# Split operands for the second half of group 1's output projections in a fused attention and FFN kernel

## The chip, the cores and the metric

One core of a Trainium2 chip runs the whole program. The metric is the device time of one execution in microseconds (us); three runs of the kernel before gave a median of 738.64 us (738.53 to 738.88). Engines are called as the profile calls them: PE (TensorE matmul), PEld (its weight load), DVE (VectorE), ACT (ScalarE), POOL (GpSimd), SP (SyncE, which issues the DMAs).

## The reference, cut to what matters

Attention over 4 batches of 8 heads, 768 positions, head size 64, where a query sees a window of 128 positions and 4 sink positions. Its output, as 3072 tokens of 512 features, goes through a feed-forward block:

```
h  = x @ w_in                      # 3072x512 @ 512x2048
sp = maximum(h, 0) + log1p(exp(-abs(h)))
g  = h * erf(sp)
out = g @ w_out                    # 3072x2048 @ 2048x512, float32
```

All inputs and the output are float32.

## The kernel before, in words

**Tiling.** The tokens are cut into 12 groups of 256 (`GT`), each group two halves of 128. `DF` = 2048 is cut into 16 blocks `f` of 128 (`NF` = 16). One step `m` is one block of one group: `g, f = divmod(m, NF)`, so group 0 is m = 0 to 15, group 1 is 16 to 31, group 2 begins at 32. In each step `hidden` (L638) makes h for block f (contraction over four c of 128 features), on odd steps `act` (L650) turns two blocks of h into g, and `project` (L678) adds the block of step m - `LAG` (`LAG` = 4) to the two output accumulators of its group.

**Attention** runs ahead of the feed-forward work in steps `s`, four head pairs to a group, one about every four m. A step is `core(s)` (L302: `av` of step s - 2, then the scores), softmax on DVE and ACT (`norm`, L371), `ptrans(s)` (L391: transposes on PE, copies on ACT, masks on POOL) and `xfin` (L459), which writes slice c of the group's x as xh (rounded) and xl (rest). So group g's four slices become complete one after another, and the last, c = 3, lets the hidden matmuls of that group finish.

**Two ways to multiply in float32.** Unsplit operands are float32 and a product is one `matmul` of the program (two instructions in the profile: L641, L687). Split operands are pairs of type float32r, a rounded part and the rest, and a product is three matmuls (L645; L690, L691, L692). Weights arrive as `ws`, are rearranged to float32 `wf` on DVE (`wconv`, L533) and are split into `wt` by `wsplit` (L555): a copy on ACT (L560) makes the rounded part, a subtraction on DVE (L561) the rest. Blocks 0 to 15 are of w_in, 16 to 31 of w_out. Group 0's hidden products are unsplit, those of all other groups split. The projections of groups 0 and 1 are unsplit (`whole` in `act`), those of groups 2 to 11 are split. For a split projection `act` ends with a cast on DVE (L674, gh) and a subtraction on POOL (L675, gl); for an unsplit one it ends with the float32 tile gf.

**What sets the order.** Each engine executes its own list in order. A planner makes these lists when the program is built: it takes ready instructions by a key, 256 times the step plus an offset by kind (`O`, L45: `act` -400, `core` -300, `ptrans` -200, `hid` 0, `ws` 300, `res` 500, `proj` 900; smaller goes first), so projections are what PE takes when nothing else is ready. `follow` (L278) adds an order between two instructions of one engine. `split` (L520) says at which m each weight block is split; L559 puts the split behind the last square and the last product of an earlier `act`. `project` gets a function (L602) that orders the first matmul of a *split* projection behind the last hidden matmul of the same step m, where that step's group is 2 or more and f is not 0. The unsplit branch (L686 to L688) does not use it. Hidden blocks 2k and 2k + 1 share one PSUM bank; the trace has the second one's matmuls behind the first one's.

**Buffers that matter here.** `g` has 2 (gf or gh with gl), `u` 4, PSUM `h`, `o` and `t` 2 each, the weights share 33.

Of the kernel before, what the change touches and what calls it, by code (L numbers as in the profile page):

```python
# [39 lines left out]
NE, AL = 4, 2  # L40

NM, NA = 2, 8

PW, EA = 256, 12
O = dict(prep=-100, norm=-100, core=-300, av=-300, load=-400, dup=-100, kcopy=-50, ptrans=-200, xfin=-100,  # L45
# [7 lines left out]
def kernel(  # L53
# [17 lines left out]
    NF = DF // P  # L71
# [59 lines left out]
    def fast_path():  # L131
        with ExitStack() as st:
# [145 lines left out]
            def follow(prev, ins):  # L278

                if prev is not None:  # L280
                    tc.add_manual_dep(
                        ins.ins, prev.ins.name,
                        mybir.DependencyInfo(mybir.DependencyClass.NoSync, mybir.DependencyReason.DATA), reason="order",
                    )
                return ins
# [188 lines left out]
            def at(a, what):  # L474

                key = int(a * PW) + O[what] + (E.get(what, 0) if a < EA else 0)
                return tc.high_priority(offset=tc.tile_snap_priority() + 1 - key)

            def pos(s):

                return s if s < NE else 3 * s - 6 if s < 2 * NPAIR else 4 * s - 11

            plan = {}
            for s in range(NSTEP + AL):
# [15 lines left out]
                if s < 2 * NPAIR:  # L500
                    x = pos(s) + (3 if s < NE else 5)
# [6 lines left out]
            def attn(a):  # L508

                for what, fn, s in sorted(plan.get(a, ()), key=lambda x: (STAGES.index(x[0]), x[2])):  # L510
                    with at(a, what):
                        fn(s)
# [3 lines left out]
            def need(n):  # L516
                return 4 * (n // 4) if n < 16 else n - 16 + LAG

            order = sorted(range(32), key=need)
            split = {}  # L520
            for n in range(32):
                split.setdefault(NF - 5 + n if n < 16 else 2 * NF - 8 + (n - 16) * 3 // 2, []).append(n)

            def wload(n):

                src = wblock(n)
                t = staged[n] = wpool.tile([P, 2 * DM], I32, tag="wo", name=f"ws_{n}")
                if src.dtype == F32:
                    nc.sync.dma_start(t[:, :DM].bitcast(F32), src)
                else:  # L530
                    nc.sync.dma_start(t, src.bitcast(I32))

            def wconv(n, wn):  # L533

                s = staged.pop(n)
                if wn % 2 == 0:
                    wpair.append(wpool.tile([P, 2, DM], F32, tag="wo", name=f"wf_{n}"))
                t = wf[n] = wpair[-1][:, wn % 2]
                if wblock(n).dtype == F32:
                    nc.vector.tensor_copy(t, s[:, :DM].bitcast(F32))  # L540
                    return
                w, ti = s.rearrange("p (n t) -> p n t", t=2), t.bitcast(I32)
                first = nc.vector.tensor_scalar(
                    ti, w[:, :, 1], 0x07FFFFFF, 3, op0=ALU.bitwise_and, op1=ALU.logical_shift_left
                )
                follow(mark["s", 2] if wn < 1 else mark["t", 3] if wn < 3 else mark["s", 3], first)
                follow(mark.get(("c", wn - 2)), first)
                nc.vector.scalar_tensor_tensor(
                    out=ti, in0=w[:, :, 1], scalar=-0x40000000, in1=ti, op0=ALU.bitwise_and, op1=ALU.bitwise_or
                )  # L550
                mark["c", wn] = nc.vector.scalar_tensor_tensor(
                    out=ti, in0=w[:, :, 0], scalar=29, in1=ti, op0=ALU.logical_shift_right, op1=ALU.bitwise_or
                )

            def wsplit(n, m):  # L555

                t = wf[n]
                d = wt[n] = wpool.tile([P, 2, DM], F32R, tag="wo", name=f"wt_{n}")
                x, y = mlp.mark[(m - 1) // 2 - 1]  # L559
                follow(x, nc.scalar.copy(d[:, 0, :], t))  # L560
                follow(y, nc.vector.tensor_tensor(d[:, 1, :], t, d[:, 0, :].bitcast(F32), op=ALU.subtract))  # L561

# [6 lines left out]
            mlp = make_mlp(work, ps_h, ps_o)  # L569
            wn, wl = 0, W0  # L570
            gs = {}
# [15 lines left out]
            for m in range(-LEAD, NG * NF + LAG + 2):  # L587
                a = m + LEAD
                live = 0 <= m < NG * NF
                if live:  # L590
                    g, f = divmod(m, NF)
                    if f % 2 == 0:
                        hp = mlp.hid_tile(m)
                    if f > 0:
                        with at(a, "hid"):
                            ahead = mlp.hidden(hp, xp[g], f)
                attn(a)
                w = m - LAG
                if 0 <= w < NG * NF:
                    g2, f2 = divmod(w, NF)  # L600
                    with at(a, "proj"):
                        mlp.project(gs[w // 2], g2, f2, lambda ins: follow(ahead if live and f and g >= 2 else None, ins))  # L602
                    if f2 == NF - 1:
                        for i in range(2):
                            r0 = (g2 * 2 + i) * P
                            with at(a, "res"):
                                nc.sync.dma_start(out[r0 : r0 + P, :], mlp.result(g2, i))
                if live:
                    if f == 0:
                        with at(a, "hid"):  # L610
                            mlp.hidden(hp, xp[g], f)
                    if f % 2 == 1:
                        with at(a, "act"):
                            gs[m // 2] = mlp.act(hp, m, g < 2)

                while wn < 32 and a >= 1 and (wn < (0, 0, 3, 5)[a - 1] if a < 5 else wn < 2 * a - 4 or need(order[wn]) <= m + W1):
                    with at(a, "wc"):
                        wconv(order[wn], wn)
                    wn += 1
                    with at(a, "wl"):  # L620
                        for n in order[wl : wn + WQ]:
                            wload(n)
                            wl += 1
                for n in split.get(m, ()):
                    with at(a, "ws"):
                        wsplit(n, m)
# [72 lines left out]
    def general_path():  # L699

        NT_S = S // P
        with ExitStack() as st:
# [71 lines left out]
            with tc.tile_pool(name="g_one1", bufs=1) as one, tc.tile_pool(name="g_work1", bufs=2) as work:  # L774
# [3 lines left out]
                with tc.For_i(0, B, 1) as b:  # L778
                    for gb in range(GPB):
# [25 lines left out]
                        for i in range(2):  # L805
# [3 lines left out]
                            )  # L809

    fast_path()
    ok = nc.values_load(flagi[0:1, 0:1], min_val=0, max_val=1)
    with tc.If(ok == 0):  # L813
# [31 lines left out]
```

## Time and profile before

| | value |
|---|---|
| median of 3 runs | 738.64 us (738.53 to 738.88) |
| profiled execution, device time | 738.16 us |
| its span in the trace | 736.5 us (1.66 us lie around it) |
| PE busy | 716.0 us, 97% |
| PEld busy | 595.6 us, 81% |
| ACT busy | 551.9 us, 75% |
| DVE busy | 485.3 us, 66% |
| POOL busy | 210.1 us, 29% |
| mean granted PE clock | 0.997 |

A matmul's listed duration contains its pipeline and overlaps the next one; what one costs in a row of them is the distance between starts. The profiled execution is 0.48 us below the median of the runs.

### The profile page before, as it was taken

How to read it: one execution, taken by the hardware profiler on the slowest of the kernel's cores; microseconds unless marked ns; L12 is line 12 of the kernel's file. 1: busy time of each engine (PE TensorE's matmuls, PEld its weight loads, DVE VectorE, ACT ScalarE, POOL GpSimd, SP SyncE). 2: the span in 40 equal slices, each digit the busy share in tenths (PEclk: the TensorE clock that was granted, in tenths of full speed). 3: DMA queues.
4: the chain of work that ended last, by engine and by line, in shares of the span. 5: the costliest groups of instructions: out<-in, count | busy, mean ns of one | idle time of the engine just before them, and what ended most of it. 6: DMA issues, size and time to landing. Idle time of an engine off the chain costs nothing. (4 is left out here: it accounts for less than half of the span.)

```text
span 736.5 us, 16405 instructions
## 1 busy us (share of the span) xinstructions
PE 716.0 (97%) x5808; PEld 595.6 (81%) x5808; DVE 485.3 (66%) x1367; ACT 551.9 (75%) x1313; POOL 210.1 (29%) x302
## 2 busy tenths in 40 slices
PE   6889999999999999999999999999999999999997
PEld 3666567767888888888888888888898888898885
DVE  7999997665776765665666666665566566475252
ACT  4687759976986876976976975985886886777573
POOL 3411332111323322332333232233224223233221
PEclk9999999999999999999999999999999999999999
DMA  7999011121222122212212211311321221200000
GB/s 175 279 347 377 22 37 55 31 57 40 72 48 69 45 54 48 65 43 57 67 41 56 75 38 44 84 36 40 78 48 37 79 58 35 67 13 2 29 1 34
DMA packets 113001, 53.07 MB, mean 72 GB/s; under 512 B 91728, under 2 KB 105552, under 8 KB 112912
## 3 DMA queue, kind: packets, MB, share of 16 engines
q1 hardware_dynamic: 112352, 51.87, 26.3%
q8 instruction: 49, 0.80, 0.5%
q14 instruction: 40, 0.33, 0.1%
q10 hardware_dynamic: 560, 0.07, 0.1%
HBM read 38.01 MB, written 6.29 MB: 60 GB/s over the span
## 5 line engine op out<-in xcount | busy, mean ns | idle before, releaser
L645 PE MATMUL h<-xh,wt 128*128 128x256 f32 x1408 | 277.9, 285 | 0.2 <-DVE u L667 0.2
L645 PEld LDWEIGHTS h<-xh,wt 128*128 128x128 f32 x1408 | 224.0, 188 | 7.6 <-issue 1.7
L675 POOL TENSOR_TENSOR g<-u,g 128x512 fp32r<-128x512 f32 x80 | 106.2, 1327 | 339.3 <-DVE g L674 335.4
L645 PE MATMUL h<-xl,wt 128*128 128x256 f32 x704 | 198.2, 282 | 0.0
L663 ACT ACTIVATE u<-r 128x512 f32<-128x512 f32 x288 | 161.5, 622 | 12.7 <-DVE gf L667 4.7
L645 PEld LDWEIGHTS h<-xl,wt 128*128 128x128 f32 x704 | 132.2, 188 | 5.0 <-issue 1.2
L667 DVE SCALAR_TENSOR_TENSOR u<-u,u 128x512 f32<-128x512 f32 x160 | 124.5, 778 | 16.0 <-ACT u L663 1.8
L691 PE MATMUL o<-wt,g 128*128 128x512 f32 x320 | 127.4, 398 | 0.0
L690 PE MATMUL o<-wt,g 128*128 128x512 f32 x320 | 127.3, 398 | 0.0
L692 PE MATMUL o<-wt,g 128*128 128x512 f32 x320 | 123.6, 397 | 0.2 <-POOLq L813 0.2
L667 DVE SCALAR_TENSOR_TENSOR u<-u,h 128x512 f32<-128x512 f32 x80 | 54.9, 686 | 84.5 <-ACT u L663 82.3
L416 POOL TENSOR_SCALAR_AFFINE_SELECT pz<-pa 64x256 f32<-64x256 f32 (+1 forms) x96 | 54.5, 567 | 150.8 <-ACT pa L405 147.5
L367 ACT ACTIVATE pst<-pst,neg 128x144 f32<-128x144 f32 x192 | 77.4, 407 | 24.9 <-DVE neg L363 23.9
L658 ACT ACTIVATE r<-h 128x512 f32<-128x512 f32 x96 | 56.7, 591 | 17.9 <-PE h L645 14.4
L690 PEld LDWEIGHTS o<-wt,g 128*128 128x128 f32 x320 | 60.0, 187 | 11.5 <-ACT ot L696 0.4
L692 PEld LDWEIGHTS o<-wt,g 128*128 128x128 f32 x320 | 59.0, 188 | 12.5 <-POOLq L813 0.7
L691 PEld LDWEIGHTS o<-wt,g 128*128 128x128 f32 x320 | 60.0, 188 | 10.5
L674 DVE CAST g<-u 128x512 fp32r<-128x512 f32 x80 | 34.6, 432 | 46.3 <-PE o L692 43.6
L659 ACT ACTIVATE r<-r 128x512 f32<-128x512 f32 x96 | 60.7, 632 | 2.5
L660 ACT ACTIVATE r<-r 128x512 f32<-128x512 f32 x96 | 60.7, 632 | 2.5
L687 PE MATMUL o<-wf,gf 128*128 128x512 f32 x128 | 58.3, 594 | 1.2 <-DVE gf L667 1.2
L297 ACT COPY kq<-tqk 128x512 f32<-128x512 f32 x48 | 27.9, 582 | 32.6 <-PE tqk L294 30.2
(88 smaller groups left out, 939.2 us busy)
## 6 DMA issues: line engine op xcount, KB each, us to landing
ws<-in_moe_w_in_dram SPq DMA_DIRECT2D x16, 512.0 KB, 6.0
ws<-in_moe_w_out_dram SPq DMA_DIRECT2D x16, 512.0 KB, 8.3
out_dram<-ot SPq DMA_DIRECT2D x24, 256.0 KB, 2.1
v<-in_v_dram SPq DMA_DIRECT2D x56, 96.0 KB, 2.2
q<-in_q_dram SPq DMA_DIRECT2D x80, 64.0 KB, 2.1
k<-in_k_dram SPq DMA_DIRECT2D x80, 64.0 KB, 2.1
vz<-v SPq DMA_DIRECT2D x80, 64.0 KB, 2.1
kq<-kq SPq DMA_DIRECT2D x28, 64.0 KB, 2.0
```

What stands on the lines that cost most here:

```text
L367: nc.scalar.activation(y, y, AF.Exp, bias=d["neg"][:, i, h : h + 1], scale=-1.0, accum_out=d["sum"][:, i, h : h + 1])
L645: last = nc.tensor.matmul(o, wt[NC * j + c][:, p, fs], xt[e][:, c, :], start=(m == 0), stop=(m == len(ops) - 1))
L658: nc.scalar.activation(r, h, AF.Tanh, bias=b_t, scale=0.5)
L659: nc.scalar.activation(r, r, AF.Square, bias=b_v, scale=-0.5)
L660: nc.scalar.activation(r, r, AF.Square, bias=b_r)
L663: sq = nc.scalar.activation(u, r, AF.Square, bias=b_a[i], scale=CS)
L667: pr = nc.vector.scalar_tensor_tensor(out=acc, in0=u, scalar=CC[i] * CS**2, in1=x, op0=ALU.add, op1=ALU.mult)
L675: nc.gpsimd.tensor_tensor(gl, acc, gh.bitcast(F32), op=ALU.subtract)
L687: nc.tensor.matmul(o, gt[0][:, ws], wf[16 + f], start=(f == 0), stop=(f == NF - 1))
L690: behind(nc.tensor.matmul(o, gh[:, ws], wt[16 + f][:, 0, :], start=(f == 0), stop=False))
L691: nc.tensor.matmul(o, gh[:, ws], wt[16 + f][:, 1, :], start=False, stop=False)
L692: nc.tensor.matmul(o, gl[:, ws], wt[16 + f][:, 0, :], start=False, stop=(f == NF - 1))
```

## The change

Group 1's activations of blocks f = 8 to 15 (m = 25, 27, 29, 31) give split operands, and the projections of these blocks, done at m = 28 to 35, use the split weights 24 to 31. The eight blocks 24 to 31 are split first, at m = 22, 23, 24, 25, 27, 28, 29, 30; blocks 16 to 23 at m = 31, 31, 32, 33, 33, 34, 35, 35, all behind the activation of m = 31 or an earlier one. Before, blocks 16 to 31 were split in order at m = 24, 25, 27, 28, 30, 31, 33, 34, 36, 37, 39, 40, 42, 43, 45, 46. The splits of blocks 0 to 15 keep their places (m = 11 to 26).

```diff
 NM, NA = 2, 8
+
+FH = 8
...
             for n in range(32):
-                split.setdefault(NF - 5 + n if n < 16 else 2 * NF - 8 + (n - 16) * 3 // 2, []).append(n)
+                x = n - 16
+                split.setdefault(NF - 5 + n if x < 0 else NF + 6 + (x - FH) * 5 // 4 if x >= FH else 2 * NF - 1 + x * 2 // 3, []).append(n)
...
                 t = wf[n]
                 d = wt[n] = wpool.tile([P, 2, DM], F32R, tag="wo", name=f"wt_{n}")
-                x, y = mlp.mark[(m - 1) // 2 - 1]
+                x, y = mlp.mark[min((m - 1) // 2, NF) - 1]
                 follow(x, nc.scalar.copy(d[:, 0, :], t))
...
                     if f % 2 == 1:
                         with at(a, "act"):
-                            gs[m // 2] = mlp.act(hp, m, g < 2)
+                            gs[m // 2] = mlp.act(hp, m, m < NF + FH)
```

## Rows read from the trace of the kernel before

**Rows 1.** Windows: us, busy and count of PE, PEld, DVE, ACT, POOL, PEclk, DMA, GB/s.
```profile
160.00:174.00 14.00, 14.00 (x87) 7.82 (x86) 5.21 (x18) 5.37 (x18) 1.42 (x5) 1.00 0.18 41
174.00:190.00 16.00, 14.53 (x131) 12.63 (x130) 10.58 (x43) 15.36 (x43) 2.68 (x6) 1.00 0.36 93
```

**Rows 2.** Waits of PE, 120 to 215 us (three) and 215 to 736 us (one).
```profile
PE av L453 <- ACT pz L411: 0.7, 1, 0.7
PE tp L398 <- DVE pst L382: 0.5, 1, 0.5
PE h L645 <- DVE u L667: 0.2, 1, 0.2
...
PE o L692 <- POOLq L813: 0.2, 1, 0.2
```

**Rows 3.** Timeline of PE: unsplit projections of group 1, and what follows them.
```profile
130.51 7.03 PE L687 MATMUL o<-wf,gf 128*128 128x512 f32 x16
137.38 0.60 PE L398 MATMUL tp<-ident,pst 128*128 128x128 f32 x4
```

**Rows 4.** Timeline of PE: first of 16 split projection matmuls, and what follows them.
```profile
203.80 0.40 PE L691 MATMUL o<-wt,g 128*128 128x512 f32 x1
...
207.53 0.28 PE L645 MATMUL h<-xh,wt 128*128 128x256 f32 x1
```

**Rows 5.** Timeline of PE where group 1 ends: scores 12, projections, av 11, scores 13 and 14.
```profile
157.67 0.85 PE L345 MATMUL ps<-kq 64*64 64x144 f32 x16
...
168.37 3.60 PE L687 MATMUL o<-wf,gf 128*128 128x512 f32 x8
171.90 0.67 PE L453 MATMUL av<-pa,v 128*64 128x64 f32 x12
...
172.96 0.85 PE L345 MATMUL ps<-kq 64*64 64x144 f32 x16
...
180.38 0.85 PE L345 MATMUL ps<-kq 64*64 64x144 f32 x16
```

**Rows 6.** Timeline of PE where group 2 ends: av 15, first projection behind group 3's hidden matmuls.
```profile
226.89 0.55 PE L453 MATMUL av<-pa,v 128*64 128x128 f32 x8
...
232.78 0.40 PE L690 MATMUL o<-wt,g 128*128 128x512 f32 x1
```

**Rows 7.** Source lines: count, duration ns min/median/max, first and last start.
```profile
L560 ACT CAST wt<-wf x32: 600/612/634, 89.4 to 209.6; 128x512 fp32r<-128x512 f32 x32
...
L561 DVE TENSOR_TENSOR wt<-wf,wt x32: 676/685/901, 92.7 to 211.3; 128x512 fp32r<-128x512 f32 x32
...
L674 DVE CAST g<-u x80: 410/427/528, 183.3 to 727.5; 128x512 fp32r<-128x512 f32 x80
...
L675 POOL TENSOR_TENSOR g<-u,g x80: 1278/1295/1672, 183.9 to 728.1; 128x512 fp32r<-128x512 f32 x80
```

**Rows 8.** Timeline of ACT where group 1 ends; idle before in brackets.
```profile
160.31 1.12 ACT L560 CAST wt<-wf 128x512 fp32r<-128x512 f32 x2
...
161.91 0.42 ACT L367 ACTIVATE pst<-pst,neg 128x144 f32<-128x144 f32 x1
...
168.51 0.59 ACT L405 COPY pa<-tp 128x512 f32<-128x512 f32 x1 [4.90 <-PE tp L398]
```

**Rows 9.** Timeline of DVE where group 1 ends; idle before in brackets.
```profile
163.65 0.17 DVE L374 TENSOR_SCALAR sum<-sum 128x4 f32<-128x4 f32 x1 [3.32 <-ACT pst L367]
...
165.31 0.28 DVE L386 TENSOR_TENSOR snk<-pst,sum 128x128 f32<-128x128 f32 x1
...
173.49 0.42 DVE L472 TENSOR_TENSOR xl<-av,xh 128x256 fp32r<-128x256 f32 x1 [5.37 <-ACT xh L471]
```

**Rows 10.** Timelines of DVE and POOL: four softmax scalings without and with POOL's subtraction beside them.
```profile
177.18 0.88 DVE L382 TENSOR_SCALAR pst<-pst,sum 128x128 f32<-128x128 f32 x4
...
206.41 1.93 DVE L382 TENSOR_SCALAR pst<-pst,sum 128x128 f32<-128x128 f32 x4
...
206.37 1.30 POOL L675 TENSOR_TENSOR g<-u,g 128x512 fp32r<-128x512 f32 x1 [3.28 <-DVE sum L375]
```

## The prediction

> **What bounds the kernel now.** I read the windows first. Where group 1 ends, PE is busy for the whole 14.00 us of the stretch 160 to 174 while ACT and DVE work 5.37 and 5.21 us; in the next 16 us PE is busy 14.53 us and ACT, with 15.36 us, is nearly full [rows 1]. The granted clock is 1.00, the 2.4 GHz level, in both. Next come the waits: from 120 to 215 us PE waited three times, 0.7, 0.5 and 0.2 us, 1.4 us together and all of it between 174 and 190, and from 215 to 736 us it waited 0.2 us [rows 2]. So from 120 us on the time is PE's work. What PE no longer has to do comes off the end, unless it waits more elsewhere, and after 215 us nothing is there to take it back. The question is the stretch 150 to 190, where the change lies. Last I read the timeline of that stretch, because there the order of the lists can open a wait that no total shows.
>
> **PE: the products themselves.** 16 instructions of the unsplit form took from 130.51 to 137.38, 0.429 us each, and a product is two of them: 0.859 us [rows 3]. 16 of the split form took from 203.80 to 207.53, 0.233 us each, and a product is three: 0.699 us [rows 4]. The change turns 8 blocks times 2 halves, 16 products, from the one to the other: 16 x 0.160 = **2.55 us** less. All of it lies in the part where PE has no wait, so I count it in full.
>
> The Trainium skill gives other spacings: by "FP8 and Floating Point Precision", section TensorE Precision Notes, true FP32 takes 4 passes, and by "TensorE: Matmul & The Clock Gate", section Back-to-back issue gap, an isolated matmul of 512 columns takes about 216 ns. An estimate from these two pages is 16 x (4 - 3) x 0.216 = 3.5 us less. The rows agree for the unsplit form (0.859 against 0.864) and not for the split one (0.699 against 0.648), so the sum goes by the rows.
>
> **DVE, ACT and POOL: what is added.** Four activations get a cast on DVE, 0.427 us, and a subtraction on POOL, 1.295 us [rows 7]: 1.7 and 5.2 us. POOL is busy 1.42 us in 160 to 174 [rows 1], so its part is hidden unless the projection stands right behind it. It comes three to four steps behind its activation (`LAG`), so it does not; only the last pair (f = 14, 15) is close, and that pair is moved later (below). No split is added; all 32 stay. But 21 of them now lie in m = 22 to 35 instead of 13, that is 8 casts of 0.61 us on ACT and 8 subtractions of 0.69 us on DVE [rows 7], 4.9 and 5.5 us by their durations, taken out of m = 36 to 46. Three of the eight come in among group 1's activations (m = 22 to 30 hold 13 splits instead of 10), where PE had no wait that they could lengthen [rows 1, 2]; five come in behind the last of them (m = 31 to 35 hold 8 instead of 3). There ACT stood idle 4.90 us before its copy at 168.51 [rows 8], and DVE 3.32 and 5.37 us [rows 9]. That is the cover, and I cost the move at nothing; without cover it is the third rival. In return ACT, 15.36 of 16 us busy in 174 to 190, loses casts there. No DMA is added or moved, and the SP queue is as before.
>
> One row speaks against more work for POOL: the four scalings of a softmax step took 0.88 us alone and 1.93 us when POOL's subtraction began at the same moment [rows 10]. So each of the four new subtractions may cost DVE 0 to 1.06 us. The Trainium skill has this as a rule ("SBUF — State Buffer", section Who interferes with whom): a DVE instruction in a two-port mode and a GpSimd instruction block each other for a whole instruction. The trace agrees. On the path it costs 0, or 1.06 us if one hits the softmax of step 12; I take 0, as DVE has 8.7 us of idle time around it [rows 9].
>
> **PE: the order, which is the real risk.** A split projection's first matmul goes behind the last hidden matmul of its step if that step's group is 2 or more and f is not 0. For f = 13, 14, 15 of group 1 the steps are m = 33, 34, 35, that is hidden blocks 1 to 3 of group 2. Unsplit they were free of this. Before, f = 14 and 15 were done from 168.37 on [rows 5] and f = 13 shortly ahead, while nothing else was ready until step 11's av (171.90), which gives the last slice of group 2's x. After the change they cannot be done until that slice is there. So PE loses work with which it bridged that wait. How long is the hole? The round from scores 12 (157.67) to scores 13 (172.96) lasted 15.3 us and PE was busy throughout [rows 1, 5]. Take out three unsplit blocks (3 x 1.72 = 5.2) and the saving of f = 10 to 12 (3 x 0.32 = 1.0): PE has 9.1 us of work left in it. What else must pass in that round is softmax, transposes, copies, av. The next round, 13 to 14, did the same in 7.4 us [rows 5]; then there is no hole. As round 12 ran, the sums came at 163.65 [rows 9], late because ACT did two split casts at 160.31 ahead of the exponentials at 161.91 [rows 8]. The last scaling ended at 165.6 [rows 9], 7.9 us after the scores. Behind it stand the transposes (0.60 [rows 3]), the copies on ACT (0.59 for the first [rows 8], I take twice that for all) and av (171.90 to 172.96, 1.06 [rows 5]), 2.9 us, with handovers 3.1 as an estimate: 11.0 us from scores to scores, a hole of 1.9 us. So **0 to 1.9 us**. The boundary of groups 2 and 3 has this same order already: the blocks behind group 3's hidden matmuls begin at 232.78, after av 15 at 226.89 [rows 6], and PE has no wait there [rows 2]. That pulls towards 0, ACT's casts towards 1.9; I take 0.9.
>
> **PE: what comes back.** The three blocks, now 3 x 1.40 = 4.2 us, are done after the last slice, in 174 to 190, where PE waited 1.4 us [rows 2] for a chain through ACT and DVE that now also has fewer splits beside it. Between 0 and 1.4 us come back; as three times as much work as wait is put there, I take 0.8.
>
> **One wait is added behind this.** Group 1's accumulators are finished later, so their two copies on ACT (like the copy of 0.59 us [rows 8]) come closer to group 2's first projection, which needs those banks. Behind that projection PE still has hidden matmuls of the next pair; 0 to 1.2 us, taken as 0.
>
> **The sum.** 2.55 - 0.9 + 0.8 = 2.45 us less. The profiled execution, 738.16 us (a span of 736.5 and 1.66 around it), would become 735.7. It is 0.48 us under the median of the runs, 738.64, so against the median I forecast **736.2 us**, 0.33% less.
>
> **The rivals.** *The waits go too* (chance 0.12): no hole, and all 1.4 us of waits vanish: 738.64 - 2.55 - 1.4 = 734.7. For it speaks that the split projections no longer hold a `g` buffer from the first product on, only from the cast, so PSUM tiles come free earlier. Against it: those waits are for a softmax chain that is no shorter.
>
> *The hole eats it* (0.20): hole 1.9 us, nothing comes back: 738.0, and with half of the accumulator wait 738.6. For: two casts stood ahead of exponentials before, and more casts are in that stretch now. Then the change does not do what it says in effect: PE works 2.55 us less and waits as much longer, no difference. Against: rows 6.
>
> *Splits in front of the softmax* (0.08, slower): the eight casts of blocks 16 to 23 become ready together behind the last activation. If ACT's list has them ahead of step 12's exponentials or its copies (rows 8 show two so placed), av 11 comes later by 0.56 us each, with nothing left for PE. All eight, 4.5 us on top of the 1.9, give 738.64 - 2.55 + 6.4 = 742.5. It is slower than now once hole and casts pass 2.55 us, and measurably so, past 740.1, beyond 4.0 us, when four of the eight stand there. Against: their key is the largest of those on ACT except the result copies, so they go in only when nothing else is ready in the planner's clock.
>
> **How the numbers follow.** The forecast has 0.60, with its own range 735.0 to 737.2 (hole 0 to 1.9, back 0 to 1.4, not both at the bad end). Two runs of this kernel can be told apart from about 0.2%, 1.48 us: below 737.16 is faster, above 740.12 slower. Faster is 0.60 + 0.12 and 0.02 of the second rival, 0.74; same 0.18; slower 0.08. For 8 in 10 the range reaches from the first rival's full gain to the second's end, 734.4 to 738.6; the third rival, the edge of the second and a gain beyond the first stay out.
>
> **What would show it.** Right: 96 L687 instructions instead of 128, 336 instead of 320 of each of L690 to L692, 84 casts at L674; PE busy about 2.5 us less; the blocks f = 13 to 15 after group 2's first hidden matmuls; L560 ending by about 175 us instead of 209.6; no PE wait after 215 us. The hole would be a wait of PE on L453 or L398, released by ACT or DVE, between 160 and 172. Wrong: a PE wait there of over 2 us with casts L560 ahead of L367 or L405 on ACT (third rival), split products at another spacing than 0.233 us, or new waits at later group boundaries.

## The result and the profile after

The changed kernel takes 744.1 us (median of 4 runs, 743.07 to 744.9) against 738.59 us of the kernel before on the same chip: ratio 1.0072, 95% interval 1.006 to 1.0085. It is **slower by 5.5 us**, where 736.2 was forecast and 738.6 was the end of the range. The profiled execution, 743.62 us with a span of 742.0, stands for it.

The page says what was computed and not where the time is: PE is busy 715.8 us (716.0 before), although 16 products went to the cheaper form. The windows place it (us, busy and count of PE, PEld, DVE, ACT, POOL, PEclk, DMA, GB/s):

```profile
150.00:160.00 10.00, 10.00 (x60) 8.70 (x59) 9.28 (x25) 9.73 (x25) 1.97 (x2) 1.00 0.26 57
160.00:174.00 14.00, 8.68 (x68) 6.28 (x66) 7.82 (x28) 5.49 (x18) 3.44 (x6) 0.76 0.18 40
174.00:190.00 16.00, 15.76 (x157) 13.68 (x158) 7.24 (x24) 12.69 (x33) 4.62 (x11) 0.89 0.31 82
190.00:210.00 20.00, 20.00 (x167) 18.04 (x167) 13.61 (x43) 15.49 (x38) 5.79 (x8) 1.00 0.20 45
```

Two things answer to [rows 1]: PE idles 5.3 us in 160 to 174, where it had no idle time, and the granted clock falls to 0.76 and 0.89, a mixture of the two levels, 2.4 and 1.2 GHz. Who is waited for, as in [rows 2] (PE, 120 to 215 us; total, times, longest):

```profile
PE tp L400 <- DVE pst L384: 4.4, 2, 2.5
PE av L455 <- ACT pz L413: 0.7, 1, 0.7
PE av L455 <- ACT pa L407: 0.5, 1, 0.5
```

After 215 us PE waits 0.2 us, as before. PE's timeline gives the order, to be read against [rows 5]; the scores of step 11 began at 148.75 (144.69 before):

```profile
148.75 0.99 PE L347 MATMUL ps<-kq 64*64 64x208 f32 x16
...
160.00 0.63 PE L695 MATMUL o<-wt,g 128*128 128x512 f32 x2
163.13 1.02 PE L400 MATMUL tp<-ident,pst 128*128 128x128 f32 x4 [2.50 <-DVE pst L384]
...
164.82 1.12 PE L455 MATMUL av<-pa,v 128*64 128x64 f32 x12 [0.46 <-ACT pa L407]
...
166.73 1.50 PE L347 MATMUL ps<-kq 64*64 64x144 f32 x16
...
172.48 0.89 PE L400 MATMUL tp<-ident,pst 128*128 128x128 f32 x4 [1.92 <-DVE pst L384]
...
176.15 1.44 PE L347 MATMUL ps<-kq 64*64 64x144 f32 x16
...
181.55 0.40 PE L693 MATMUL o<-wt,g 128*128 128x512 f32 x1
```

At 160.6 PE has done every projection it may do (up to f = 12; f = 13 to 15 begin at 181.55, as the order rule wants). But attention is not one round from the end of group 2's x, as forecast, but two: the transposes at 163.13 are those of step 11, whose turn was 153.02 before, and the scores of step 12 come at 166.73 instead of 157.67. PE stands before both rounds with nothing else to do, and part of what it does there runs at the lower level of the clock: from av to the first hidden matmuls behind it 4.11 us (164.82 to 168.93) and 3.68 us (174.25 to 177.93), against 2.26 before (171.90 to 174.16).

Why attention is late is seen in ACT's and DVE's lists. Step 10's exponentials on ACT, before (they began at 131.52, ahead of the three casts):

```profile
131.52 0.41 ACT L367 ACTIVATE pst<-pst,neg 128x144 f32<-128x144 f32 x1 [0.45 <-DVE neg L363]
...
134.68 1.64 ACT L560 CAST wt<-wf 128x512 fp32r<-128x512 f32 x3
```

and after the change (behind the squares of an activation and three casts; four casts had gone at 126.91, where three had):

```profile
126.91 2.17 ACT L563 CAST wt<-wf 128x512 fp32r<-128x512 f32 x4
...
131.83 1.67 ACT L666 ACTIVATE u<-r 128x512 f32<-128x512 f32 x3
133.41 1.64 ACT L563 CAST wt<-wf 128x512 fp32r<-128x512 f32 x3
134.95 0.41 ACT L369 ACTIVATE pst<-pst,neg 128x144 f32<-128x144 f32 x1
```

The row maxima that the first of these exponentials needs were there at 132.3, before the three casts began. On DVE step 10's scalings, which began at 134.71 before the change, then stood behind three subtractions of splits as well:

```profile
136.69 0.17 DVE L376 TENSOR_SCALAR sum<-sum 128x4 f32<-128x4 f32 x1 [1.36 <-ACT pst L369]
...
137.37 0.69 DVE L564 TENSOR_TENSOR wt<-wf,wt 128x512 fp32r<-128x512 f32 x1
...
138.06 1.26 DVE L564 TENSOR_TENSOR wt<-wf,wt 128x512 fp32r<-128x512 f32 x2
139.24 0.87 DVE L384 TENSOR_SCALAR pst<-pst,sum 128x128 f32<-128x128 f32 x4
```

Step 11's softmax on DVE after the change: three subtractions of splits stand between its sums (159.42) and its scalings (162.71), and the pair of them that took 2.27 us ran beside POOL's new subtraction, which began at 160.06 and lasted 1.58 us:

```profile
159.42 0.16 DVE L376 TENSOR_SCALAR sum<-sum 128x4 f32<-128x4 f32 x1
159.50 0.42 DVE L677 CAST g<-u 128x512 fp32r<-128x512 f32 x1
159.83 0.68 DVE L564 TENSOR_TENSOR wt<-wf,wt 128x512 fp32r<-128x512 f32 x1
160.43 0.17 DVE L377 RECIPROCAL sum<-sum 128x4 f32<-128x4 f32 x1
160.52 2.27 DVE L564 TENSOR_TENSOR wt<-wf,wt 128x512 fp32r<-128x512 f32 x2
162.71 0.86 DVE L384 TENSOR_SCALAR pst<-pst,sum 128x128 f32<-128x128 f32 x4
```

The two delays come from different splits. The last eight of the 32 subtractions, by the order of the steps those of blocks 16 to 23, begin at 152.20. So step 10 was held up where blocks 24 to 31 crowd in among the last of blocks 0 to 15, and step 11, late already, was held up further by blocks 16 to 23.

**An account.** The activation of m = 17 starts 0.36 us earlier than before (108.92 against 109.28), that of m = 49 5.53 later (237.29 against 231.76), the last 5.54 later (728.00 against 722.46). So 5.9 us are lost between 109 and 237 us and nothing after it. Of these, idle time of PE from 120 to 200 us is 5.57 - 1.47 = 4.1 us, the products give back 2.55, and 4.35 us are left: PE at the lower clock. That last figure is a remainder; the two stretches above give 3.3 us of it, and e12 below tests it. Up to m = 17 the lists of all sixteen kernels of this document are the same, and yet that activation starts between 108.87 and 111.02 us in their profiled executions: a difference of up to 2 us between two of these can come from ahead of it.

### The profile page after: what moved, and what is told of

It is laid out like the page before. It is cut to its first block, busy times and chain, and to the rows that moved or that the text cites. A ratio compares the mean times of both kernels' runs of the same rounds, so it can differ in the third digit from the quotient of the medians.

```text
span 742.0 us, 16461 instructions
## 1 busy us (share of the span) xinstructions
PE 715.8 (96%) x5824; PEld 600.5 (81%) x5824; DVE 489.9 (66%) x1371; ACT 553.5 (75%) x1313; POOL 213.8 (29%) x306
## 5 line engine op out<-in xcount | busy, mean ns | idle before, releaser
L678 POOL TENSOR_TENSOR g<-u,g 128x512 fp32r<-128x512 f32 x84 | 111.3, 1325 | 370.1 <-DVE g L677 369.6
L670 DVE SCALAR_TENSOR_TENSOR u<-u,u 128x512 f32<-128x512 f32 x168 | 133.5, 795 | 14.8
L694 PE MATMUL o<-wt,g 128*128 128x512 f32 x336 | 133.8, 398 | 0.0
L693 PE MATMUL o<-wt,g 128*128 128x512 f32 x336 | 133.6, 398 | 0.0
L695 PE MATMUL o<-wt,g 128*128 128x512 f32 x336 | 130.2, 397 | 0.2 <-POOLq L816 0.2
L670 DVE SCALAR_TENSOR_TENSOR u<-u,h 128x512 f32<-128x512 f32 x84 | 57.7, 687 | 83.1 <-ACT u L666 80.9
L693 PEld LDWEIGHTS o<-wt,g 128*128 128x128 f32 x336 | 63.0, 187 | 12.0 <-ACT ot L699 0.4
L695 PEld LDWEIGHTS o<-wt,g 128*128 128x128 f32 x336 | 62.0, 187 | 13.2 <-POOLq L816 0.7
L694 PEld LDWEIGHTS o<-wt,g 128*128 128x128 f32 x336 | 63.0, 188 | 11.0
L677 DVE CAST g<-u 128x512 fp32r<-128x512 f32 x84 | 36.7, 436 | 50.3 <-PE o L695 47.2
L407 ACT COPY pa<-tp 128x512 f32<-128x512 f32 x48 | 28.1, 585 | 29.2 <-PE tp L400 29.1
```

The lines of the kernel that those rows point to most:

```text
L670: pr = nc.vector.scalar_tensor_tensor(out=acc, in0=u, scalar=CC[i] * CS**2, in1=x, op0=ALU.add, op1=ALU.mult)
L678: nc.gpsimd.tensor_tensor(gl, acc, gh.bitcast(F32), op=ALU.subtract)
L693: behind(nc.tensor.matmul(o, gh[:, ws], wt[16 + f][:, 0, :], start=(f == 0), stop=False))
L694: nc.tensor.matmul(o, gh[:, ws], wt[16 + f][:, 1, :], start=False, stop=False)
L695: nc.tensor.matmul(o, gl[:, ws], wt[16 + f][:, 0, :], start=False, stop=(f == NF - 1))
```

## The experiments

Two theories stood after the result: **A**, the order rule takes PE's bridge away; **B**, splits ahead of the softmax make attention late. Times are medians; the kernel before had 738.4 to 738.7 us beside them. All edits are against the changed kernel unless said otherwise.

**e1: the places of the splits alone.**

```diff
-                            gs[m // 2] = mlp.act(hp, m, m < NF + FH)
+                            gs[m // 2] = mlp.act(hp, m, g < 2)
```

> The changed places of the weight splits alone: every projection of group 1 stays unsplit (4 fewer casts on DVE, 4 fewer subtractions on POOL, 16 products back to 0.859 us). Theory A (the order rule: PE waits because f = 13 to 15 may not be done before group 2's hidden blocks): unsplit projections are free of that rule, so no hole, scores of step 12 near 158 us as before, 738.6 us, 738 to 739.3. Theory B (the splits: ACT's and DVE's lists have more of them ahead of the softmax of steps 10 and 11, so attention comes late): scores of step 12 at 163 us or later as in the changed kernel (166.7), PE bridges part of it with 6.9 us more work than the changed kernel had there, 739 to 741 us.

742.17 us, ratio 1.0044 (1.0027 to 1.0062), more than either theory gave. Scores of step 12 at 167.57, where B wanted 163 or later and A 158. So splits alone make attention late. The longer, free projections bridge most of it (longest wait of PE 0.8 us, clock 1.00 throughout), and it is slower all the same: between the activations of m = 17 and 49 it loses 2.2 us, and PE idles 3.3 us from 120 to 210 us, where it idled 1.5. Another 1.7 us of its profiled execution lie ahead of m = 17.

**e2: the order rule taken off group 1's split projections.**

```diff
-follow(ahead if live and f and g >= 2 else None, ins)
+follow(ahead if live and f and g >= 2 and g2 >= 2 else None, ins)
```

> The changed kernel without the order rule for group 1's split projections (f = 13 to 15 need no longer follow hidden blocks 33 to 35). A: the 4.2 us of these three blocks bridge the wait, waits of PE between 150 and 190 fall from 5.6 us to under 1.5, clock stays at 1.00, 735.5 to 737.5 us. B: attention is as late as before, scores of step 12 near 166 us, and 4.2 us of work only cover part of the waits and of the clock's fall: 738 to 741 us.

741.67 us, 1.0046 (1.0028 to 1.0063): as B had it, though beyond its 741 us. Scores of step 12 at 167.75. The freed blocks bridge the first wait, and then nothing is left for the second: PE goes into step 11's transposes (165.41) without a wait and waits 2.49 us ahead of step 12's.

```profile
165.41 0.60 PE L400 MATMUL tp<-ident,pst 128*128 128x128 f32 x4
...
172.39 0.89 PE L400 MATMUL tp<-ident,pst 128*128 128x128 f32 x4 [2.49 <-DVE pst L384]
```

The clock is 0.89 in 174 to 190. The rule is worth 2.4 us here; without it 3.3 us of loss remain, so it is not the cause of these.

**e3: the order rule alone, in the kernel before** (its unsplit projections get it too).

```diff
-nc.tensor.matmul(o, gt[0][:, ws], wf[16 + f], start=(f == 0), stop=(f == NF - 1))
+behind(nc.tensor.matmul(o, gt[0][:, ws], wf[16 + f], start=(f == 0), stop=(f == NF - 1)))
```

> The kernel before with the order rule put on its unsplit projections too (f = 13 to 15 of group 1 behind hidden blocks 33 to 35), nothing else. A: a hole of 2 us or more ahead of step 11's av and a clock below 1.00 behind it, 740 to 742 us. B: attention is not late, PE finds other work, 738.3 to 739.3 us.

742.63 us, 1.0058 (1.0041 to 1.0075), near A's 740 to 742 us, but lost in another place. Ahead of step 11's av, PE waited only 0.82 us and the av came earlier (167.40 against 171.90). The loss came a group later, ahead of step 15's av: PE's timeline has

```profile
227.25 1.03 PE L398 MATMUL tp<-ident,pst 128*128 128x128 f32 x4 [2.62 <-DVE pst L382]
```

and a clock of 0.89 in 210 to 240. So neither A nor B told it: the planner answered the rule with other lists.

**e4: blocks 16 to 23 later, one per step** (m = 31 to 38, behind their own step's activation).

```diff
-NF + 6 + (x - FH) * 5 // 4 if x >= FH else 2 * NF - 1 + x * 2 // 3
+NF + 6 + (x - FH) * 5 // 4 if x >= FH else 2 * NF - 1 + x
...
-                x, y = mlp.mark[min((m - 1) // 2, NF) - 1]
+                x, y = mlp.mark[(m - 1) // 2 - 1]
```

> The changed kernel with blocks 16 to 23 split one per step at m = 31 to 38, behind the activations of their own step, instead of two or three per two steps right behind group 1's last activation. A: nothing of the order rule is touched, 743 to 745 us. B: fewer subtractions stand in DVE's list inside step 11's softmax (the scalings came 3.1 us after the sums), the wait of 2.5 us before the transposes shrinks by 1 to 2 us: 741 to 743 us.

740.41 us, 1.0029 (1.0019 to 1.0039): 3.7 us better than the change, more than B hoped. Step 11's scores are as late as in the change (149.87), those of step 12 come at 163.94 instead of 166.73. One wait of 2.5 us is left, ahead of step 12's transposes, and the clock is 0.83 and 0.93. So moving blocks 16 to 23 alone, with the first eight as crowded as before, takes back two thirds of the loss.

**e5 and e6: one split per step everywhere**, with the rule and without it (e6 also has e2's edit).

```diff
-NF + 6 + (x - FH) * 5 // 4 if x >= FH else 2 * NF - 1 + x * 2 // 3
+NF + 2 + x if x >= FH else 2 * NF + x
...
-                x, y = mlp.mark[min((m - 1) // 2, NF) - 1]
+                x, y = mlp.mark[(m - 1) // 2 - 1]
```

> The changed kernel with one weight split per step and no crowding: blocks 24 to 31 at m = 26 to 33, blocks 16 to 23 at m = 32 to 39, each behind the activation of its own step. The order rule stays. B (splits delay the softmax of steps 10 and 11): step 10's softmax sees no split more than before, so the scores of step 11 return to about 145 to 146 us and those of step 12 to about 158; what is left is the order rule. A and B together then give a hole like that of the order rule alone (e3, 742.6) less 2.55 us of products: 739 to 740.5 us. If the splits were all of it: 736 to 737 us.

> As e5, and without the order rule for group 1's split projections. If the loss is the splits ahead of the softmax plus the order rule and nothing else, PE keeps its 2.55 us: 735.5 to 736.8 us, waits of PE from 97 to 240 us at most 2 us, clock 1.00 throughout. If something else in the split operands costs (the casts on DVE, POOL's subtractions beside the scalings), attention is late still: 738 to 741 us.

e5: 741.01 us, 1.0026 (1.0014 to 1.0037), where 740.5 was the most expected; e6: 741.89, 1.0041 (1.0028 to 1.0054). Step 11's scores are back in time (145.6 and 144.6), as B said, but step 12's are late again (162.5, 161.5). e5 has a wait of 2.84 us ahead of step 12's transposes and a clock of 0.87. e6 has none over 1.0 us and the clock at 1.00 up to 240 us, its activation of m = 49 starts 3.29 us *earlier* than before, and it still ends late. e6's time was a miss for both theories, and e14 is about it.

**e7: e4 without the rule.**

> e4 (blocks 16 to 23 one per step at m = 31 to 38; blocks 24 to 31 crowded as in the changed kernel) without the order rule for group 1. Step 10 and 11 stay late because of the crowded first eight, so the three blocks freed bridge only part: between e4 (740.4) and e6, 737.5 to 739.5 us. If the crowded first eight are harmless: as e6, 735.5 to 736.8 us.

740.82 us, 1.0028 (1.0018 to 1.0039), worse than expected: no better than e4. With the first eight blocks crowded the scores of steps 11 and 12 are late (150.1, 165.9). The rule makes no difference to the time here, where it made 2.4 us between the change and e2.

**e8: e5's places, everything unsplit.**

> The places of e5 for the splits with all of group 1's projections unsplit (control for e1): B says places that don't crowd steps 10 and 11 cost nothing, 738 to 739 us, scores of step 11 at about 145 us against 151.5 in e1. If any delay of the split order costs: 740 to 742 us as e1.

745.03 us, 1.0079 (1.0061 to 1.0097). Scores of step 11 at 144.8 and of step 12 at 159.0, in time, no hole, clock 1.00, and yet 6.4 us slower, beyond both ranges. Like e6 it loses behind group 1.

**e9 and e10: the places as changed, but each of these splits behind a softmax in the lists**, with the rule (e9) and without (e10: also e2's edit).

```diff
-                        nc.scalar.activation(
+                        mark["e", s] = nc.scalar.activation(
...
-                follow(x, nc.scalar.copy(d[:, 0, :], t))
-                follow(y, nc.vector.tensor_tensor(d[:, 1, :], t, d[:, 0, :].bitcast(F32), op=ALU.subtract))
+                s = None if n < 16 else 10 if m < 25 else 11 if m < 31 else 12
+                follow(mark.get(("e", s)), follow(x, nc.scalar.copy(d[:, 0, :], t)))
+                lo_part = nc.vector.tensor_tensor(d[:, 1, :], t, d[:, 0, :].bitcast(F32), op=ALU.subtract)
+                follow(mark.get(("s", s)), follow(y, lo_part))
```

> The changed kernel, places of the splits and order rule as changed, but each split of blocks 16 to 31 put behind a softmax in both lists: the cast behind the last exponential, the subtraction behind the last sink scaling of step 10 (m = 22 to 24), 11 (m = 25 to 30) or 12 (m = 31 to 35). B (splits in the lists ahead of the softmax make attention late, and that is the loss): scores of step 11 at 144 to 146 us (148.8 as changed, 144.7 before), those of step 12 at 156 to 159 us (166.7 as changed), waits of PE from 120 to 200 us at most 2.5 us, clock 1.00 throughout: 736 to 738.5 us. A (the order rule is what counts): it is still there, so the hole stays: 740 to 744 us.

> As e9, and without the order rule for group 1's split projections. If both causes are needed to lose time, nothing is gained over e9: 735.5 to 738 us, within 1 us of e9. If the rule alone opens a hole (A): 736 us, with e9 at 740 or more.

e9: 740.16 us, 1.002 (1.001 to 1.003); e10: 738.34 us, 0.9996 (0.9986 to 1.0005), no different from before. Both have step 11's scores early (144.0, 142.4) and step 12's in time (158.1, 156.5), as B expected. The times are neither theory's: e9 is in A's range and not in B's, and e10 is neither within 1 us of e9 nor at 736. This single edit is worth 3.9 us (744.1 to 740.16), and the rule another 1.8. e9 also shows the hole that the prediction had sized: PE's timeline has

```profile
168.66 0.39 PE L650 MATMUL h<-xh,wt 128*128 128x256 f32 x1 [2.02 <-DVE u L672]
...
173.73 0.50 PE L650 MATMUL h<-xh,wt 128*128 128x256 f32 x2 [1.31 <-ACT xh L473]
175.30 0.38 PE L650 MATMUL h<-xl,wt 128*128 128x256 f32 x1 [1.06 <-DVE xl L474]
```

The last two are waits for the last slice of group 2's x, 2.4 us together (0 to 1.9 were forecast). The first is new: PE's bank is freed late by DVE's product, because the subtractions now crowd DVE. Three of them, from 166.11, stand ahead of that product, and three more, from 171.96, ahead of the subtraction that makes xl (174.83), so part of the 2.4 us is theirs too.

**e11 and e13: e10 and e9 with blocks 16 to 23 one per step at m = 32 to 39** (behind their own step's activation; those before m = 36 also behind step 12's softmax). e11 is without the rule, e13 with it. The split of e9's edit, and:

```diff
-NF + 6 + (x - FH) * 5 // 4 if x >= FH else 2 * NF - 1 + x * 2 // 3
+NF + 6 + (x - FH) * 5 // 4 if x >= FH else 2 * NF + x
...
-                x, y = mlp.mark[min((m - 1) // 2, NF) - 1]
+                x, y = mlp.mark[(m - 1) // 2 - 1]
...
+                s = None if n < 16 else 10 if m < 25 else 11 if m < 31 else 12 if m < 36 else None
```

> e10 (splits of blocks 16 to 31 behind a softmax, no order rule for group 1), with blocks 16 to 23 split one per step at m = 32 to 39, behind the activation of their own step, so that DVE (12.4 of 14 us busy in 160 to 174 in e10) has fewer subtractions ahead of the products that free PE's banks. If what e10 still loses (2.6 us of PE waits from 120 to 200 us, on DVE's products and on xh) is DVE's load there: waits at most 1.5 us, 736 to 737.5 us, faster than the kernel before. If it is the softmax chain itself, PE having too little else to do: 737.8 to 738.8 us as e10.

> e11 with the order rule for group 1's split projections put back, nothing else. If the rule costs by itself where attention is in time (PE has no work left ahead of step 11's av, as between e10 and e9, 1.8 us): 736.5 to 738 us, with waits of PE on xh or xl between 160 and 175 us. If it costs only where attention is late: 735 to 736 us as e11.

e11: **735.22 us**, ratio 0.9957 (0.9941 to 0.9974), faster than both kernels and than expected; e13: 735.78 us, 0.9961 (0.9947 to 0.9975), as expected if the rule costs only where attention is late. e13 has the change's split products and its order rule and differs from it only in where the splits stand: 744.1 against 735.78 us. So with products and rule alike the place of the splits in the lists makes the whole loss, and once it is put right the forecast's 736.2 us comes out within half a microsecond. The rule alone is worth some half a microsecond, less than the two intervals can tell apart. All of e13's waits of PE from 120 to 215 us:

```profile
PE h L650 <- DVE u L672: 0.8, 1, 0.8
PE o L697 <- POOL g L680: 0.2, 1, 0.2
```

e11's windows beside [rows 1]:

```profile
160.00:174.00 14.00, 13.73 (x121) 11.60 (x120) 11.16 (x42) 11.32 (x34) 5.22 (x7) 1.00 0.28 61
174.00:190.00 16.00, 15.37 (x129) 13.22 (x128) 12.07 (x32) 15.74 (x39) 4.34 (x7) 1.00 0.33 88
```

Idle time of PE is 0.9 us in e11, where it was 1.5 before, and between the activations of m = 17 and m = 49 it gains 3.06 us on the kernel before (0.14 to 3.20 us earlier). That is the forecast's 2.55 and a part of the old waits.

**e12: the hole filled with idle work.** 22 transposes of the identity ahead of the transposes of steps 11 and 12, into a tile that these overwrite.

```diff
+                if s in (11, 12):
+                    prev = None
+                    for _ in range(22):
+                        prev = follow(prev, nc.tensor.transpose(out=tp[:, 0, 0, :], in_=ident, identity=ident))
```

> The changed kernel with 22 transposes of the identity ahead of the transposes of steps 11 and 12 each, into the tile that these then overwrite: about 4.7 us of PE work more at the full clock, which serves nothing but to keep PE busy where it waited; nothing else is changed. If the fall of the clock behind the wait (0.76 in 160 to 174, 0.89 in 174 to 190) cost about 4 us of its own: clock 1.00 there and, though PE does more, 740 to 742.5 us. If only the wait counts: the work fits into the wait or adds to it, 743.5 to 748 us.

741.13 us, 1.0037 (1.0023 to 1.0052): **3.0 us faster by doing more.** The two blocks took 2.56 us each, one at 152.80, one in the second hole:

```profile
152.80 2.56 PE L401 MATMUL tp<-ident 128*128 128x128 f32 x22
...
167.71 2.56 PE L401 MATMUL tp<-ident 128*128 128x128 f32 x22
170.83 0.89 PE L404 MATMUL tp<-ident,pst 128*128 128x128 f32 x4
```

The granted clock is 1.00 in every window from 60 to 690 us, and scores 13 follow scores 12 after 7.5 us (166.19 to 173.66) instead of 9.4. Attention is as late as in the change (scores of step 12 at 166.2), so it is not the lateness that was cured. Counted by the distance between starts the two blocks cost PE 4.6 us, and PE idles 1.5 us in 160 to 190 instead of 5.6. So 4.0 us of waits went, 4.6 us of work came, and 3.0 us were gained: an estimate from these is 3.6 us for the clock, between the 3.3 us of the two stretches and the 4.35 us of the account.

**e14: e11 with unsplit projections.**

> e11 with all of group 1's projections unsplit, so that 16 products cost 0.859 instead of 0.699 us. If the lists were alike, this would be e11 plus 2.55 us: 737.8 us. But its lists of ACT from group 2 on have the other rhythm (the exponentials of a step in two parts in most steps) that e6 and e8 have and that e11 and the kernel before have not; there PE was busy 4 us longer after 215 us without a wait that the profile lists. If that rhythm is what e6 and e8 lost by: 741 to 745 us, all of the difference to the kernel before arising after 215 us.

746.46 us, 1.0099 (1.0082 to 1.0116), beyond the 745 expected. The activation of m = 17 started 1.50 us later than before, that of m = 49 0.40 earlier, the last one 7.92 later: all of the loss, and more, comes behind group 1. After 215 us the profile lists only 1.7 us of waits of PE, none of them long (the largest item, 0.8 us in all, is h waiting for DVE's u). One difference in the lists is that ACT's exponentials come in two parts in 13 of the 26 steps behind 300 us (1 of 26 in e11), as in e6 and e8. It is not the only one: from m = 65 to m = 161 the lists of PE, ACT, DVE and POOL are the same in the other thirteen kernels, the one before and the changed one among them, and each of these takes 343.16 us for that stretch; in e6, e8 and e14 all four lists are others, and it takes 345.99, 346.83 and 346.71 us. So the loss goes with these lists; which of their differences costs the time was not tried. In 300 to 690 us, where e11's first projection matmul of a product has a mean of 398 ns, e14's has 404:

```profile
L695 PE MATMUL o<-wt,g 128*128 128x512 f32 x216 | 87.4, 404 | 0.1
```

(e11's row: x221, 88.0 us.) PE does fewer of them in the same time and loses a little at many places, most of it too little at each for the list of waits. What sets the planner into this rhythm was not tried either.

## Why the prediction was wrong, point by point

**The products: right.** 22 split matmuls from 154.16 to 159.29 in the changed kernel are 0.233 us each, and L690 has 96 instructions, L693 336, L677 84 casts, as said. e11 and e13 keep the gain. The row's spacing and not the page's decided it well.

**The step that failed** stands in the part on DVE, ACT and POOL: three more splits come in "among group 1's activations (m = 22 to 30 hold 13 splits instead of 10), where PE had no wait that they could lengthen", five more "behind the last of them", where idle time of ACT and DVE was to cover them, and the move was costed at nothing. Both halves failed. The splits stand in the same lists as the softmax of steps 10 and 11. In the changed kernel the first half put step 10's exponentials behind three casts and its scalings behind three subtractions, the second put step 11's scalings behind three subtractions, and the scores of step 12 came 9.1 us later. That PE had no wait there only said that it had a bridge, namely projections; it did not say that the chain behind it had slack. And the idle time that was to be the cover (ACT's 4.90 us up to 168.51, DVE's up to 163.65 and 173.49) belongs to step 12's round; the second half's splits ran from 152.20 on, in step 11's. Taking the second half out of the way gives 3.7 us back (e4), putting all of them behind the softmax 3.9 (e9), both 8.3 (e13).

**The order rule: right in mechanism, wrong in how much of it decides.** The hole of 0 to 1.9 us was worked out for one round. Where only one round is left, it is 2.4 us of waits and 1.8 us of time in e9, and in e13, with DVE less crowded, no wait for group 2's x is listed and the rule's 0.6 us are within the noise. In the changed kernel two rounds were left, and the rule was worth 2.4 us. e2 shows that taking the rule away does not cure it.

**The clock: missing.** The text said 1.00 for both windows and priced no fall. Some 3.3 us (the two stretches) to 4.4 us (the account) were lost because PE, having waited 2.5 us, ran the attention chain at a mixture of the two levels, and this chain was just what everything waited for. That hole therefore cost more than its length. The Trainium skill tells the like of a kernel that waits for DMAs, in "TensorE: Matmul & The Clock Gate", section HAM oscillation: where PE waits between bursts, the gate falls back and the next burst starts cold. The trace agrees, 0.76 granted behind the wait.

**The rivals.** The third, splits in front of the softmax, was given 0.08. It is the nearest to what happened, but it had been put on ACT and at step 12, behind group 1's last activation. It happened one and two rounds earlier, at the softmax of steps 11 and 10, and on DVE as much as on ACT. That such splits "go in only when nothing else is ready in the planner's clock" was no protection: on the chip step 10's exponentials had their input at 132.3 and stood behind casts until 134.95, since an engine does its list in order. Where the planner's clock had that input is not on record.

**After 215 us nothing takes it back: right for the changed kernel, not in general.** Its shift stays at 5.5 us to the end. But e6, e8 and e14 lose 7.0 to 8.3 us behind m = 49, where their lists are others.

**POOL's subtraction beside DVE** cost more than the 0 taken: two subtractions of splits, some 1.3 us on their own, took 2.27 in the middle of step 11's softmax. That 1.0 us is the 1.06 that the prediction had named as the most one hit could cost, at step 11 and not at step 12. The Trainium skill names this case in "SBUF — State Buffer", section Who interferes with whom (a DVE instruction with two inputs in SBUF beside GpSimd), and the row agrees.

## What to carry to other kernels

Low-priority work that is moved into a list with a latency chain in it must be costed at that chain, not at the busy share of its engine: ask which instruction of the chain will stand behind it. An engine without waits may be running on a bridge; a change that speeds its work up and another that ties the bridge down take it away together. And where a planner makes the lists, put the order that matters into the program (here: splits behind the softmax). The edits of places without it (e1, e4 to e8) all lost 2.0 to 6.4 us. It is no guarantee: e9 has it and lost 1.6 us, e14 has it and lost 7.9 us where its lists changed far from the edit.

## What the runs showed that was not expected

The clock fell behind one long wait of PE: in the change (2.50 us), e2 (2.5), e3 (2.6), e4 (2.5) and e5 (2.8), each with a granted clock under 1.00 in the window of the wait or the next. In e9, whose longest wait was 2.0 us, and in e7, e10 and e11, with 1.3, 1.1 and 0.6, it stayed at 1.00 in every window from 60 to 690 us. More work for PE can make a kernel faster (e12: 4.6 us of work more, 3.0 us of time less). And e14 lost over 8 us behind group 1 with 1.7 us of waits in the list and the clock at 1.00.
